# Alpha as ScalarE's partition scale in a fused attention and snake MLP, in place of scaled weights

## The chip, the cores and the metric

The kernel runs on one core of one Trainium2 chip. The metric is the device time of one execution in microseconds (us), as the median of several runs. The *profiled span* is the length of one profiled execution; it is about 2 us shorter than the time of the same run. Line numbers (L372) belong to the kernel whose profile is shown: L489 of the kernel before and L472 of the changed one are the same matmul.

## The reference

```python
# attention with keys and values averaged over 8 rows, 8 batches, 8 heads, 576 rows, head 64
scores = scale * q @ mean8(k).T;  attn = softmax(scores);  x = attn @ mean8(v)     # x: 4608 x 512
# the MLP: w_in 512 x 2048, w_out 2048 x 512, alpha: 2048
h = x @ w_in
s = sin(alpha * h)
g = h + s * s / (alpha + 1e-9)
out = g @ w_out
```

All is float32. Alpha belongs to a column of h; in the kernel h lies transposed, so alpha belongs to a partition.

## The kernel before

Both matmuls of the MLP are cut into 2x2 blocks and done with seven products in place of eight (a Strassen form), which needs sums of blocks of x, w_in and w_out. The first matmul runs in nine *units* of 512 tokens. A unit has four groups J of seven products, 28 *slots*; in each slot the instructions listed for it go ahead of that slot's product on every engine, and the attention of the next batch is laid into the slots this way. The second matmul (the *output stage*) follows from about 560 us to the end.

The kernel before folds alpha into the weights. With w_in' = w_in * alpha the product is alpha*h at once. The sine then needs alpha/(alpha + 1e-9), and w_out is divided by alpha + 1e-9, so that the square can be plain.

```python
    def combine_alpha(self):
        ...                                  # al: alpha by partition
        for c in range(4):                   # alb: alpha in the free dimension, on all partitions
            nc.tensor.matmul(ps[:], self.ones[:], self.al_row[:, s], start=True, stop=True)
            nc.scalar.activation(out=self.alb[:, s], in_=ps[:], func=AF.Identity, ...)
        # ral = 1 / (al + 1e-9),  rat = al * ral
    def combine_w_in(self, J, part):         # VectorE, in slots of the first unit (J = 0: before it)
        def scaled(t, i):
            nc.vector.tensor_tensor(out=t[:, :, s], in0=t[:, :, s], in1=c, op=OP.mult)    # L372
        ...                                  # four scaled() and four sums for each J
    def load_w_out(self, wp):
        ...
                    nc.vector.tensor_scalar(out=t[:, k], in0=t[:, k], scalar1=self.ral[:, f:f + 1], ...)  # L408
    # one group's pieces, run one slot behind its products 1, 5, 6, 2, 7, 3, 4
            def left0(G=G, Q=before):        # after product 1
                nc.scalar.copy(out=G.b6[:], in_=G.b1[:])                    # L507
                if Q and not early(Q):
                    squares(Q)               # of the group before: 128x512 and 128x1024
            ...
            def left2(G=G, Q=before):        # after product 6
                nc.scalar.copy(out=G.b7[:], in_=G.b6[:])                    # L519
                nc.scalar.copy(out=G.p5[:], in_=G.b5[:])
            def left3(G=G):
                sin(G, 0, 0, G.b1)
                square(G, G.s[:, 0, 0])
            ...
```

The copies L507 and L519 put a partial sum into the bank to which a later product adds: TensorE waits for them if they are late. Five banks rotate.

## Time and profile before

| | kernel before |
|---|---|
| time | 958.22 us (957.25 to 960.15) |
| profiled span | 956.4 us |
| busy: TensorE, VectorE, ScalarE, GpSimd | 937.6, 676.5, 414.2, 197.7 us |
| values matmul of the first batch begins | 34.62 us |
| second unit's long stretch begins | 130.03 us |
| from unit to unit after that | 57.20 us |
| output stage begins | 560.43 us |

The prediction below shows the rows of this profile that it rests on. Two views are needed beside them. The first is the chain of waits in the steady part (start, length, what; x144 is the number of matmuls). Each unit from the second on has one stretch of 18 products, 144 matmul records, with nothing of the attention between them; it serves as a clock mark:

```profile
187.23 31.32 PE bank L489 x144
...
462.11 45.17 PE bank L489 x208
...
560.43 4.62 PE bank L752 x40
```

187.23 less the 130.03 of the unit before is 57.20, the length of a unit. The second view is TensorE's timeline between 40 and 100 us, of which these are the matmuls that waited (start, length, what, and in brackets the wait and what ended it):

```profile
44.41 1.97 PE L489 MATMUL bank<-home,as 128*128 128x256 f32 x8 [1.64 <-DVE as L368]
...
49.48 1.99 PE L489 MATMUL bank<-home,a 128*128 128x256 f32 x8 [1.39 <-ACT bank L519]
...
55.75 0.44 PE L177 MATMUL ps_kt<-ident,kp 72*128 72x72 f32 x4 [0.81 <-ACT aT L269]
...
80.92 1.99 PE L489 MATMUL bank<-home,as 128*128 128x256 f32 x8 [1.00 <-ACT bank L507]
...
97.39 1.14 PE L267 MATMUL ps_at<-ident,ex 128*72 128x128 f32 x8 [2.02 <-DVE aT L269]
```

With the wait of 1.62 at 89.89, which the prediction shows, the six come to 8.5 us.

### The profile page before, as it was taken

The page shows a single profiled execution, that of the slowest core. Times are in us where ns is not written, and L with a number is a line of the kernel's source. Part 1 is how long each engine was busy: PE and PEld are TensorE (multiplying, and loading weights), DVE is VectorE, ACT ScalarE, POOL GpSimd, SP SyncE. Part 2 cuts the span into 40 slices and gives each one's busy share as a digit, 9 for nine tenths or more (in the row PEclk, how much of TensorE's full clock was granted, in tenths as well). Part 3 has the DMA queues.
Part 4 walks back from the last instruction along what each step waited for, and adds up shares of the span by engine and source line. Part 5 has one row for each costly group of instructions (what it writes and reads, how often), then busy time and mean ns, then how long its engine had stood idle before and what let it go on. Part 6 is the DMA issues. An engine that isn't in the chain of part 4 may idle for free.

```text
span 956.4 us, 18152 instructions
## 1 busy us (share of the span) xinstructions
PE 937.6 (98%) x7259; PEld 833.4 (87%) x7259; DVE 676.5 (71%) x1070; ACT 414.2 (43%) x919; POOL 197.7 (21%) x215
## 2 busy tenths in 40 slices
PE   7998999999999999999999999999999999999998
PEld 3677687887878878787888899999999999999998
DVE  5889585766838577483576996867768695958684
ACT  5376466575756747566555531111111111111111
POOL 1717364443724436260000000000000000000000
PEclk9999999999999999999999999999999999999999
DMA  9636466666576663745615235324142434343201
GB/s 222 176 104 198 125 195 142 205 149 196 171 198 201 156 190 102 188 136 161 242 54 206 98 142 190 125 102 161 67 155 78 143 115 147 98 139 122 100 34 35
DMA packets 84038, 137.88 MB, mean 144 GB/s; under 512 B 10177, under 2 KB 49873, under 8 KB 79345
## 3 DMA queue, kind: packets, MB, share of 16 engines
q1 hardware_dynamic: 83920, 136.70, 47.1%
q8 instruction: 58, 0.95, 0.4%
q14 instruction: 26, 0.21, 0.1%
q10 hardware_dynamic: 34, 0.02, 0.0%
HBM read 74.47 MB, written 47.19 MB: 127 GB/s over the span
## 4 chain that ended last, share of the span: by engine, by line
PE 92%; DVE 4%; ACT 2%; DMA 1%; issue 0%; SPq 0%; DVEq 0%; ACTq 0%
PE bank L489 42%; PE bank L752 30%; PE ps_y L752 12%; PE ps_o L309 3%; PE ps_sc L208 2%; DMA q<-in_q_dram 1%; DVE as L368 1%; ACT s L495 1%; PE ps_at L267 1%; DVE home L462 1%; DVE a L372 1%; PE ps_qt L189 1%; PE bank L452 1%; DVE h L468 0%; PE ps_or L318 0%
## 5 line engine op out<-in xcount | busy, mean ns | idle before, releaser
L489 PE MATMUL bank<-home,a 128*128 128x256 f32 x1152 | 266.3, 382 | 3.0 <-DVE h L468 1.6
L489 PEld LDWEIGHTS bank<-home,a 128*128 128x128 f32 x1152 | 215.3, 190 | 36.6 <-DVE h L468 3.1
L489 PE MATMUL bank<-home,as 128*128 128x256 f32 x864 | 201.6, 382 | 2.8 <-DVE as L368 1.6
L489 PEld LDWEIGHTS bank<-home,as 128*128 128x128 f32 x864 | 161.7, 190 | 26.7 <-ACT bank L507 2.4
L105 POOL TENSOR_TENSOR kvin<-kvin 72x512 f32<-72x512 f32 x112 | 126.0, 1125 | 180.3 <-DMA kvin<-in_v_dram 112.0
L495 ACT ACTIVATE s<-h,rat 128x256 f32<-128x256 f32 x144 | 65.2, 500 | 90.2 <-DVE h L468 90.2
L468 DVE TENSOR_TENSOR h<-bank,p 128x512 f32<-128x512 f32 x72 | 49.1, 682 | 74.7 <-ACT s L497 47.4
L752 PE MATMUL bank<-wb,home 128*128 128x128 f32 x712 | 92.1, 275 | 0.0
L752 PEld LDWEIGHTS bank<-wb,home 128*128 128x128 f32 x712 | 85.7, 192 | 0.0
L831 ACT COPY bank<-bank 128x128 f32<-128x128 f32 x63 | 15.8, 250 | 149.3 <-PE bank L752 149.2
L497 ACT ACTIVATE s<-s 128x512 f32<-128x512 f32 (+1 forms) x106 | 77.8, 768 | 1.1
L495 ACT ACTIVATE s<-bank,rat 128x256 f32<-128x256 f32 x144 | 59.9, 467 | 36.9 <-PE bank L489 24.4
L752 PE MATMUL bank<-wb,xe 128*128 128x128 f32 x512 | 67.6, 275 | 0.0
L752 PEld LDWEIGHTS bank<-wb,xe 128*128 128x128 f32 x512 | 62.4, 192 | 0.1
L844 ACT COPY bank<-bank 128x128 f32<-128x128 f32 x63 | 15.8, 250 | 96.6 <-PE bank L752 96.6
L250 POOL TENSOR_TENSOR ex<-ex,sm 128x576 f32<-128x576 f32 (+1 forms) x38 | 42.5, 1148 | 46.5 <-DVE sm L249 21.4
L549 DVE TENSOR_TENSOR h<-h,s 128x1024 f32<-128x1024 f32 x36 | 44.5, 1237 | 0.0
L549 DVE TENSOR_TENSOR h<-bank,s 128x512 f32<-128x512 f32 x36 | 24.5, 681 | 24.5 <-ACT s L497 23.9
L819 ACT COPY bank<-ps_y 128x256 f32<-128x256 f32 x63 | 22.5, 357 | 35.9 <-PE ps_y L752 35.9
L519 ACT COPY bank<-bank 128x512 f32<-128x512 f32 x36 | 20.6, 571 | 39.4 <-PE bank L489 39.4
L712 DVE TENSOR_TENSOR xe<-home 128x512 f32<-128x512 f32 x30 | 19.4, 687 | 25.5 <-PE bank L752 25.4
L215 DVE TENSOR_REDUCE mx<-ps_sc 128x4 f32<-128x288 f32 (+1 forms) x75 | 33.6, 448 | 4.4 <-PE ps_sc L208 4.4
(152 smaller groups left out, 1499.3 us busy)
## 6 DMA issues: line engine op xcount, KB each, us to landing
g_bridge<-h SPq DMA_DIRECT2D x36, 1024.0 KB
r<-g_bridge SPq DMA_DIRECT2D x18, 1024.0 KB
home<-g_bridge SPq DMA_DIRECT2D x18, 1024.0 KB
out_dram<-o SPq DMA_DIRECT2D x36, 256.0 KB
q<-in_q_dram SPq DMA_DIRECT2D x8, 1024.0 KB
kvin<-in_k_dram SPq DMA_DIRECT2D x28, 288.0 KB
kvin<-in_v_dram SPq DMA_DIRECT2D x28, 288.0 KB
a<-in_moe_w_in_dram SPq DMA_DIRECT2D x16, 256.0 KB
```

The costliest lines, as they stand in the source:

```text
L105: (eng or nc.gpsimd).tensor_tensor(out=o, in0=t[:, :, 0:w], in1=t[:, :, w:2 * w], op=OP.add)
L215: nc.vector.tensor_reduce(out=mx[:n], in_=ps[:n], axis=AX, op=OP.max)
L250: eng.tensor_tensor(out=E(n, i, 0, H), in0=E(n, i, 0, H), in1=sm[:n].unsqueeze(2).to_broadcast([n, H, Sp]), op=OP.mult)
L309: nc.tensor.matmul(ps[64 * e:64 * e + 64, :], vp[:, h, :], x, start=True, stop=True)
L468: add = lambda o, x, y: nc.vector.tensor_tensor(out=o, in0=x, in1=y, op=OP.add)
L489: nc.tensor.matmul(ps[:, jj, :], self.A[p][:, kk, f * P:(f + 1) * P], x[:, kk, :], start=(start and jj == 0 and kk == 0), stop=(kk == 1), ...
L495: nc.scalar.activation(out=G.s[:, i, j, jj, :], in_=src[:, jj, :], func=AF.Sin, scale=self.rat[:, f:f + 1])
L497: square = lambda G, x: nc.scalar.activation(out=x, in_=x, func=AF.Square)
L519: nc.scalar.copy(out=G.b7[:], in_=G.b6[:])
L549: add = lambda o, x, y: nc.vector.tensor_tensor(out=o, in0=x, in1=y, op=OP.add)
L752: nc.tensor.matmul(out, A[:, J, :], W[:, J // 2, J % 2, :], start=(start and J == 0), stop=(J == self.NJ - 1), skip_group_check=True)
L819: nc.scalar.copy(out=x[:, 0:2, :], in_=yz[:, 0:1, :].to_broadcast([P, 2, P]))
```

## The change

Its intent is to take 48 scalings of weights off VectorE and the spreading of alpha off TensorE, and to have ScalarE apply alpha inside instructions that it runs anyway. The sine takes alpha as its scale. The square takes c = 1/sqrt(alpha + 1e-9) as its scale, since (c*s)^2 = s*s/(alpha + 1e-9). A partition scale holds for one block of 128 columns of w_in only, so a square that went over two or four such blocks is cut. Slots move to make room.

```diff
-        # combine_alpha: four ones-by-row matmuls, four evictions into alb; ral; rat
+    def root(self):
+        ts(a, self.al[:], 1e-9, OP.add, 1.0, OP.mult)
+        nc.vector.reciprocal(out=t, in_=a)
+        nc.scalar.activation(out=c, in_=t, func=AF.Sqrt)
+        ...                                             # one Newton step: c *= 1.5 - 0.5 * c * c * a
 # combine_w_in
-        (four scaled() for each J)
+        (in the groups J = 2 and 3 the first of the four sums moves from slots 12 and 20 to slots 10 and 14,
+         where their scalings stood)
 # load_w_out
-                    nc.vector.tensor_scalar(out=t[:, k], in0=t[:, k], scalar1=self.ral[:, f:f + 1], ...)
 # a group's pieces
-   ... func=AF.Sin, scale=self.rat[:, f:f + 1])
+   ... func=AF.Sin, scale=self.al[:, f:f + 1])
-            square = lambda G, x: nc.scalar.activation(out=x, in_=x, func=AF.Square)
+            def square(G, i, js):
+                for jj in range(JW):
+                    x = G.s[:, i, js, jj, :]
+                    nc.scalar.activation(out=x, in_=x, func=AF.Square, scale=self.c[:, f:f + 1])
 # slots of the first unit
-            at(6, A.k_t)
+            at(7, A.k_t)
-                at((7, 8, 9, 11, 13)[i], A.score, i)
-                at(15 + (i + 1) // 2, A.exp, i)
-                at((16, 17, 17, 18, 19)[i], A.norm, i)
+                at((8, 9, 10, 11, 13)[i], A.score, i)
+                at((15, 16, 17, 17, 17)[i], A.exp, i)
+                at((16, 17, 18, 18, 19)[i], A.norm, i)
 # slots of the later units
-                at(8 + (i + 1) // 2, A.exp, i)
-                at(9 + (i + 1) // 2, A.norm, i)
+                at((8, 9, 10, 10, 10)[i], A.exp, i)
+                at((9, 10, 11, 11, 12)[i], A.norm, i)
 # (cut: one square moved ahead of the last sine pair in the early group; names and tiles of alpha)
```

More of the change, by code (lines that the diff above doesn't have):

```diff
@@ L321, in attention, with load_alpha, turn_alpha @@
         return SimpleNamespace(**{f.__name__: f for f in (k_t, q_t, score, exp, score_exp, norm, new_a, a_t, turn, move, values, values_rest)})
-    def load_alpha(self, row, rows):
+    def load_alpha(self, rows):
         nc = self.nc
         self.al = self.const.tile([P, self.K2], F32, name="al")
-        self.ral = self.const.tile([P, self.K2], F32, name="ral")
-        self.rat = self.const.tile([P, self.K2], F32, name="rat")
-        self.alb = self.new_tr()[:, 0:self.FF]
-        self.al_row, self.al_rows = row[0:1], rows[:self.K2]
+        self.c = self.const.tile([P, self.K2], F32, name="c")
+        self.al_rows = rows[:self.K2]
         nc.scalar.dma_start(out=self.al_rows, in_=self.alpha.rearrange("(k p) -> k p", p=P))
-        nc.scalar.dma_start(out=self.al_row, in_=self.alpha.rearrange("(o n) -> o n", o=1))
-    def combine_alpha(self):
+    def turn_alpha(self):
         nc = self.nc
@@ L340, in combine_alpha @@
         nc.scalar.copy(out=self.al[:], in_=ps[:])
-        for c in range(4):
-            s = slice(512 * c, 512 * c + 512)
-            ps = self.bank([P, 512], c)
-            nc.tensor.matmul(ps[:], self.ones[:], self.al_row[:, s], start=True, stop=True)
-            nc.scalar.activation(out=self.alb[:, s], in_=ps[:], func=AF.Identity, bias=self.ex[:, 0, 0, self.Sp:self.Sp + 1])
-        nc.vector.tensor_scalar(out=self.ral[:], in0=self.al[:], scalar1=1e-9, scalar2=None, op0=OP.add)
-        nc.vector.reciprocal(out=self.ral[:], in_=self.ral[:])
-        nc.vector.tensor_tensor(out=self.rat[:], in0=self.al[:], in1=self.ral[:], op=OP.mult)
+    def root(self):
+        nc, c = self.nc, self.c[:]
+        a, t = (self.const.tile([P, self.K2], F32, name=n)[:] for n in ("a", "t"))
+        tt = lambda o, x, y: nc.vector.tensor_tensor(out=o, in0=x, in1=y, op=OP.mult)
+        ts = lambda o, x, p, f, q, g: nc.vector.tensor_scalar(out=o, in0=x, scalar1=p, scalar2=q, op0=f, op1=g)
+        ts(a, self.al[:], 1e-9, OP.add, 1.0, OP.mult)
+        nc.vector.reciprocal(out=t, in_=a)
+        nc.scalar.activation(out=c, in_=t, func=AF.Sqrt)
+        tt(t, c, c)
+        tt(t, t, a)
+        ts(t, t, -0.5, OP.mult, 1.5, OP.add)
+        tt(c, c, t)
     def load_w_in(self):
@@ L368, in combine_w_in @@
         tt = lambda o, x, y, op: nc.vector.tensor_tensor(out=o[:, :, s], in0=x[:, :, s], in1=y[:, :, s], op=op)
-        def scaled(t, i):
-            c = self.alb[:, i * h + J * w:i * h + (J + 1) * w].unsqueeze(1).to_broadcast([P, 2, w])
-            nc.vector.tensor_tensor(out=t[:, :, s], in0=t[:, :, s], in1=c, op=OP.mult)
-        if J < 2:
-            if part == 0:
-                scaled(a11, 0)
-                scaled(a21, 1)
-                scaled(a22, 1)
-                tt(s1, a21, a22, OP.add)
-            else:
-                tt(s2, s1, a11, OP.subtract)
-                scaled(a12, 0)
-                tt(a21, a11, a21, OP.subtract)
-                tt(s4, a12, s2, OP.subtract)
-        elif part == 0:
-            for t, i in ((a11, 0), (a21, 1), (a22, 1), (a12, 0)):
-                scaled(t, i)
+        if part == 0:
+            tt(s1, a21, a22, OP.add)
         else:
-            tt(s1, a21, a22, OP.add)
             tt(s2, s1, a11, OP.subtract)
@@ L404, in load_w_out @@
             yield
-            for t, i in ((b11, 0), (b12, 0), (b22, 1), (b21, 1)):
-                for k in range(c, c + 2):
-                    f = i * kk + k
-                    nc.vector.tensor_scalar(out=t[:, k], in0=t[:, k], scalar1=self.ral[:, f:f + 1], scalar2=None, op0=OP.mult)
             s = slice(c, c + 2)
@@ L494, in sin @@
                     f = i * self.K2 // 2 + G.J * JW + jj
-                    nc.scalar.activation(out=G.s[:, i, j, jj, :], in_=src[:, jj, :], func=AF.Sin, scale=self.rat[:, f:f + 1])
-            square = lambda G, x: nc.scalar.activation(out=x, in_=x, func=AF.Square)
+                    nc.scalar.activation(out=G.s[:, i, j, jj, :], in_=src[:, jj, :], func=AF.Sin, scale=self.al[:, f:f + 1])
+            def square(G, i, js):
+                for jj in range(JW):
+                    f = i * self.K2 // 2 + G.J * JW + jj
+                    x = G.s[:, i, js, jj, :]
+                    nc.scalar.activation(out=x, in_=x, func=AF.Square, scale=self.c[:, f:f + 1])
             early = lambda G: G.J == (0 if G.u else 1)
             def squares(G):
-                square(G, G.s[:, 0, 1])
-                square(G, G.s[:, 1])
+                if not early(G):
+                    square(G, 0, 1)
+                square(G, 1, slice(0, 2))
+            self.squares = squares
             def left0(G=G, Q=before):
@@ L507, in left0 @@
                 nc.scalar.copy(out=G.b6[:], in_=G.b1[:])
-                if Q and not early(Q):
+                if Q:
                     squares(Q)
@@ L524, in left3 @@
                 sin(G, 0, 0, G.b1)
-                square(G, G.s[:, 0, 0])
+                square(G, 0, 0)
             def left4(G=G):
@@ L536, in left6 @@
                 sin(G, 0, 1, G.g[:, 0, 1])
+                if early(G):
+                    square(G, 0, 1)
                 sin(G, 1, 0, G.b7)
-                if early(G):
-                    squares(G)
             self.left = [(left0, left1, left2, left3, left4, left5, left6)[k]]
@@ L547, in finish @@
     def finish(self, Q):
-        nc = self.nc
-        add = lambda o, x, y: nc.vector.tensor_tensor(out=o, in0=x, in1=y, op=OP.add)
+        add = lambda o, x, y: self.nc.vector.tensor_tensor(out=o, in0=x, in1=y, op=OP.add)
         add(Q.g[:, 1, 0], Q.b7[:], Q.s[:, 1, 0])
@@ L559, in end_hidden @@
             f()
-        nc.scalar.activation(out=Q.s[:, 0, 1], in_=Q.s[:, 0, 1], func=AF.Square)
-        nc.scalar.activation(out=Q.s[:, 1], in_=Q.s[:, 1], func=AF.Square)
+        self.squares(Q)
         self.finish(Q)
@@ L572, in first_batch @@
         h = [self.hp.tile([P, 4 * POOL * self.D], F32, name="h") for _ in range(2)]
-        self.load_alpha(h[1][:], self.hp.tile([P, P], F32, name="s", bufs=1)[:])
-        self.combine_alpha()
+        self.load_alpha(self.hp.tile([P, P], F32, name="s", bufs=1)[:])
+        self.turn_alpha()
         for i in range(4):
             self.load_kv("k", 0, i, nc.vector, at=far[i // 2][:self.Sp, i % 2])
+        self.root()
         self.load_q(0)
@@ L858, in run @@
             make_identity(nc, ident)
-            self.ones = const.tile([1, P], F32, name="ones")
-            nc.gpsimd.memset(self.ones[:], 1.0)
             engines = {nc.tensor.engine, nc.vector.engine, nc.scalar.engine, nc.gpsimd.engine, nc.sync.engine}
```

## The prediction

> **What bounds the kernel now.** I read the page's busy shares first, then its slices:
>
> ```profile
> PE 937.6 (98%) x7259; PEld 833.4 (87%) x7259; DVE 676.5 (71%) x1070; ACT 414.2 (43%) x919; POOL 197.7 (21%) x215
> ...
> PE   7998999999999999999999999999999999999998
> ```
>
> TensorE is busy 98% of the span; 956.4 - 937.6 = 18.8 us is all the idle time it has. A change that gives TensorE no less work to do can win only there, plus the few places where "busy" hides a stalled pipe. So the second view is where that idle time lies, by stretches (columns: length, then busy us of PE, PEld, DVE, ACT, POOL):
>
> ```profile
> 0.00:25.00 25.00, 19.06 (x142) 10.08 (x143) 12.66 (x34) 13.28 (x42) 3.49 (x11) 1.00 0.90 219
> 25.00:50.00 25.00, 21.75 (x169) 15.94 (x168) 20.65 (x33) 9.98 (x31) 16.35 (x14) 1.00 0.67 189
> 50.00:75.00 25.00, 24.19 (x265) 19.44 (x264) 21.80 (x41) 16.04 (x32) 2.94 (x4) 1.00 0.37 108
> 75.00:100.00 25.00, 20.36 (x103) 16.83 (x102) 24.00 (x35) 17.70 (x31) 21.68 (x21) 1.00 0.58 165
> 100.00:150.00 50.00, 50.00 (x395) 39.79 (x393) 36.63 (x62) 30.82 (x62) 25.75 (x29) 1.00 0.52 152
> ```
>
> 14.6 us of the 18.8 are in the first 100 us; 3.5 more are the tail after 900 us. From 100 to 900 us TensorE has nothing to gain. In 75-100 VectorE is busy 24.0 of 25: there it sets the pace. Third view, the chain of waits followed back from the end, in its first 135 us (start, length, what):
>
> ```profile
> 2.48 11.04 DMA q<-in_q_dram
> ...
> 35.11 1.81 DVE a L372 x3
> ...
> 44.26 1.13 DVE a L372
> ...
> 68.34 2.40 DVE a L372 x4
> ...
> 130.03 31.32 PE bank L489 x144
> ```
>
> L372 is the scaling of w_in by alpha, which goes. It holds 1.81 + 1.13 + 2.40 = 5.3 us of the chain. Until 13.5 us the chain is the load of q; at 130 us it is pure matmul: 144 records in 31.32 us, 217 ns each, the rate of a full pipe.
>
> **What the Trainium skill says.** "ScalarE: Activation LUTs", section What ACT_TABLE_LOAD costs: each [128,1] pointer operand adds about 93 ns to an ACTIVATE, and back-to-back ones overlap by about 93 ns. The trace agrees: a sine with a pointer scale on 256 elements takes 500 ns from SBUF, where the two Square sizes below, without pointer, put 256 elements at 421. The same section gives 1283 ns for a table load and 1380 ns of drain on top; the trace has the 1283 exactly but no drain (a load at 192.00, the first exp at 193.29). The section Table sets: Exp and Sqrt are in different sets, so the new Sqrt brings loads of its own. "TensorE: Matmul & The Clock Gate", Part 1: the array starts at half rate and is let go after about 3.4 us of activity. Here the transposes of q run at 246 ns each from 14.02 (8 in 1.97 us) and at about 150 from 19.07 (4 in 0.59 us), so it woke near 18 us; the 7.2 us of one-row alpha matmuls before did not wake it (0.86 us per 512 columns throughout).
>
> **The change part by part.** The groups it touches, with busy us and mean ns:
>
> ```profile
> L495 ACT ACTIVATE s<-h,rat 128x256 f32<-128x256 f32 x144 | 65.2, 500 | 90.2 <-DVE h L468 90.2
> L497 ACT ACTIVATE s<-s 128x512 f32<-128x512 f32 x71 | 44.7, 630 | 1.1
> L497 ACT ACTIVATE s<-s 128x1024 f32<-128x1024 f32 x35 | 36.7, 1048 | 0.0
> L372 DVE TENSOR_TENSOR a<-a,tr 128x512 f32<-128x512 f32 x16 | 12.7, 842 | 0.0
> L408 DVE TENSOR_SCALAR wb<-wb,ral 128x256 f32<-128x256 f32 x32 | 8.7, 347 | 0.0
> ```
>
> *Removed, VectorE:* 16 scalings of w_in, 12.7 us, all between 35 and 84 us, where TensorE does wait; 32 scalings of w_out, 8.7 us, between 450 and 560 us, where TensorE is full: worth nothing. *Removed, TensorE:* eight records that spread alpha over the partitions, 7.2 us busy, before q is there at 13.5 us: worth nothing (the busy share will fall without gain). Their four evictions on ScalarE, 4 x 0.69 us, are also ahead of q.
>
> *Added at the start:* a Sqrt, a table load for it and one more for Exp (1.28 us each), seven tiny VectorE operations of about 0.2 us. VectorE ends the k sums at 11.4, so the root is ready near 13.1 with Sqrt's load long done: ahead of q. The Exp load falls at 16.6 to 17.9, and the first exp waited for its maximum until 17.8 anyway: 0.1 us at most.
>
> *Added on ScalarE:* squares are cut by partition scale. Per group, 630 + 630 + 1048 becomes four of 128x256 at about 500 and two of 128x512 at 630 + 93. Less overlaps, 2.2 us become about 4 x 0.41 + 2 x 0.63 = 2.9. Over 36 groups that is 24 us; ScalarE should read 435 to 445 us.
>
> *Moved:* one square goes ahead of the last sine pair, exps bunch differently, first-batch scores go one slot later and k's transpose moves from slot 6 to 7.
>
> **Does the extra ScalarE work cost in the steady part?** The tight place is the exp group, in the third unit:
>
> ```profile
> 191.39 0.59 ACT L507 COPY bank<-bank 128x512 f32<-128x512 f32 x1
> 192.00 1.28 ACT L225 ACT_TABLE_LOAD   x1
> 193.29 1.83 ACT L225 ACTIVATE ex<-ex 128x576 f32<-128x576 f32 x3
> 195.03 0.58 ACT L519 COPY bank<-bank 128x512 f32<-128x512 f32 x1
> ```
>
> The L519 copy ends at 195.61; by counting 217 ns records on from 187.23, the product that needs it starts at 195.94. In the new order the L507 copy no longer stands behind the squares, so it can begin when its product lands, about 190.95. Then: copy to 191.45, two squares to 192.75, load to 194.0, two exps to 195.2, copy to 195.7. A slack of 0.33 shrinks to about 0.2 but stays. The next eviction of that kind I get at 204.2 against a need at 204.6. I allow 0.3 us over all seven such units.
>
> **The walk through the first 100 us.** I step the same instructions on with the row durations, without the scalings.
> - To 44.2: no gain. The sums of x wait for x itself (38.9 us, from TensorE and ScalarE), so dropping three scalings before them only makes VectorE wait.
> - At 46.8 the last score tile's maximum comes 1.1 us sooner (one scaling of a12 less ahead of it), and with it its exps and the copy that frees the second product: gain 1.1.
> - 50 to 62: ScalarE is solid with copies, sines, squares and now sets the pace; with k's transpose out of slot 6, TensorE no longer waits to 55.75 for a buffer. The next group's first product starts about 57.0 instead of 59.9; longer squares then hold an eviction, and the third product starts near 63.5 to 64.1 instead of 65.9: gain about 2.
> - 66 to 82: four scalings (2.49 us) leave the score queue, but the exps now meet the squares on ScalarE; the product at 84.55 starts near 82.3 to 82.8: gain 2.
> - 84 to 97: here it pays most.
>
> ```profile
> 79.47 4.56 DVE L372 TENSOR_TENSOR a<-a,tr 128x512 f32<-128x512 f32 x4
> ...
> 89.89 1.99 PE L489 MATMUL bank<-home,a 128*128 128x256 f32 x8 [1.62 <-DVE h L468]
> ```
>
> Four scalings take 4.56 us while GpSimd works beside them; the norms and the add behind them come late, and TensorE waits. Without them the add is done near 86 and this product starts at about 86: gain 3.7.
> - 92 to 97: the last sums of w_in (4.8 us) still stand ahead of VectorE's copy of the transposed attention (done 97.25 before), and ScalarE's squares ahead of its copy. I get 94 to 94.5: gain about 3.3. From there TensorE is full as before.
>
> Sum: -3.3 at the start, +0.3 in the steady part: -3.0. The outputs from 560 us are pure TensorE and do not change. Prediction 958.2 - 3.0 = 955.2 us.
>
> **The rivals.** (1) The chain's full share is won, 5.3 us, or even the idle time of 34 to 98 us, about 8.6 us in the waits: 950 to 953. For it: VectorE is what TensorE waits for at 89.89 and 97.35. Against it: ScalarE takes over in 50-62, and no chain share is won whole when the wait behind it is close. (2) ScalarE becomes the bound in the exp groups: +0.6 us in each of 7 units gives back 4 us and the time is the same or 1 us longer, about 959. For it: slack of only 0.2 by my count. Against it: the early square and the bunched exps were evidently placed to keep that slack. (3) The clock gate: without the alpha matmuls the array wakes later, up to one window of 3.4 us at half rate, at most 1.5 us. Against it: those matmuls didn't wake it before either.
>
> **Range and chances.** Walking errors are about 2 us either way and the runs before spread over 2.9 us: 951.5 to 958. A 2% change would be 19 us, more than all of TensorE's idle time, and for a loss ScalarE would have to hold up every group by half a microsecond. Faster 0.01, same 0.98, slower 0.01.
>
> **What would show it.** VectorE near 654 us busy, ScalarE near 440, TensorE near 930 with the same span from 100 us on: units still 57.2 us apart. The matmul waits at 89.89 and 97.35 shorter or gone; 50-62 ScalarE solid. Wrong if TensorE shows new waits for ScalarE's copies between 100 and 560 us (rival 2), or if the first 34 us differ by over 1 us (rival 3).

## The result, and the profile after

| | before | after |
|---|---|---|
| time, median (range) of 4 runs each | 958.06 (957.25 to 960.15) | 953.72 (952.8 to 954.76) |
| ratio, 95% interval | | 0.9952 (0.9933 to 0.9971): within 2% |
| profiled span | 956.4 | 952.0 |
| long stretch of the second unit begins | 130.03 | 123.47 |
| from unit to unit | 57.20 | 57.45 |
| output stage begins | 560.43 | 555.81 |

The result lies inside the range, 1.5 us under the predicted 955.2. The table also shows that two terms of the sum were off: the start gained more than was predicted, and the part after it gave more back.

First the busy row of the changed kernel's page:

```profile
PE 932.7 (98%) x7251; PEld 830.2 (87%) x7251; DVE 659.0 (69%) x1025; ACT 440.2 (46%) x1026; POOL 199.7 (21%) x214
```

TensorE is still busy 98% of the span. VectorE lost 17.5 us and ScalarE gained 26.0, and the span moved by a quarter of the one and a sixth of the other: neither sum says anything of the time by itself.

Next the stretches from 25 to 100 us (length, then busy us of PE, PEld, DVE, ACT, POOL; granted clock, DMA share and GB/s), which answer to those in the prediction:

```profile
25.00:50.00 25.00, 23.73 (x183) 17.38 (x182) 19.08 (x32) 12.37 (x34) 13.92 (x14) 1.00 0.67 196
50.00:75.00 25.00, 25.00 (x265) 20.58 (x264) 20.11 (x35) 15.97 (x37) 8.42 (x8) 1.00 0.50 146
75.00:100.00 25.00, 23.18 (x123) 17.76 (x122) 20.87 (x32) 20.35 (x41) 21.73 (x22) 1.00 0.52 163
```

TensorE is busy 71.9 of these 75 us; before it was 66.3. The 5.6 us between are the start's gain, seen as idle time that has been filled. VectorE, 24.0 of 25 in the last row before, is at 20.9 there.

The timeline of TensorE shows which waits they were. These are the ones left between 40 and 100 us:

```profile
43.11 1.97 PE L472 MATMUL bank<-home,as 128*128 128x256 f32 x8 [0.79 <-DVE as L371]
...
47.06 1.99 PE L472 MATMUL bank<-home,a 128*128 128x256 f32 x8 [0.25 <-ACT bank L510]
...
80.69 1.99 PE L472 MATMUL bank<-home,a 128*128 128x256 f32 x8 [0.59 <-ACT bank L510]
...
90.93 1.14 PE L267 MATMUL ps_at<-ident,ex 128*72 128x128 f32 x8 [1.20 <-DVE aT L269]
```

They come to 2.8 us where there were 8.5. The wait for a buffer at 55.75 and the one for VectorE's add at 89.89 are gone; the product of the latter now begins at 84.26.

The chain shows what was given back after that (start, length, what):

```profile
123.47 31.57 PE bank L472 x144
...
180.93 31.57 PE bank L472 x144
...
457.06 45.17 PE bank L472 x208
...
555.81 4.73 PE bank L742 x40
```

The same 144 matmuls take 31.57 us where they took 31.32, and a unit is 180.93 - 123.47, rounded 57.45, where it was 57.20. So the lead is 6.56 us at the second unit's stretch, 5.05 at the stretch of 208, and 4.62 where the outputs begin. The 0.25 us a unit are lost in and just behind the exp group, at three weight loads that wait. In the third unit (timeline of ScalarE, and of TensorE's weight loads in the last three lines):

```profile
185.10 1.33 ACT L485 ACTIVATE s<-s,c 128x512 f32<-128x512 f32 x2
186.45 1.28 ACT L225 ACT_TABLE_LOAD   x1
187.74 1.26 ACT L225 ACTIVATE ex<-ex 128x576 f32<-128x576 f32 x2
188.91 0.58 ACT L510 COPY bank<-bank 128x512 f32<-128x512 f32 x1
...
189.53 1.59 PEld L472 LDWEIGHTS bank<-home,a 128*128 128x128 f32 x8 [0.18 <-ACT bank L510]
...
193.10 3.32 PEld L472 LDWEIGHTS bank<-home,a 128*128 128x128 f32 x16 [0.25 <-DVE h L451]
...
198.41 1.59 PEld L472 LDWEIGHTS bank<-home,as 128*128 128x128 f32 x8 [0.27 <-ACT bank L498]
```

The kernel before has one such wait in the same stretch:

```profile
199.29 3.32 PEld L489 LDWEIGHTS bank<-home,a 128*128 128x128 f32 x16 [0.18 <-DVE h L468]
```

What each costs the matmuls is seen from their begins in TensorE's timeline, counted from the first of the stretch (180.86 after, 187.16 before). Behind the first wait the next product begins at 10.51 us (191.37), where it began at 10.47 (197.63). Behind the second it is 15.80 (196.66) against 15.69 (202.85), and behind the third 19.39 (200.25) against 19.14 (206.30). So the copy of L510 accounts for 0.04 of the 0.25, VectorE's add of L451 for 0.07, and the copy of L498 for 0.14. It is the same in each of the six units.

The slack at the copy of L510 can now be estimated. It ends at 189.49, 8.56 us after the begin of the stretch in the chain; before it ended at 8.38 (195.61 - 187.23, from the lines in the prediction). It came 0.18 later and cost 0.04, so the slack of the kernel before was about 0.14 us and not 0.33. The matmul may be due at 8.71, but its weight load goes ahead of it and waits for the bank too.

Last, the begin of the output stage. In the kernel before, the chain there is matmul after matmul. In the changed one it goes by the last squares and the small copy behind them:

```profile
553.87 1.72 ACT s L485 x3
555.59 0.17 ACT bank L834
```

From the stretch that begins at 505.75 (510.81 before) to the outputs it is 50.06 us where it was 49.62, a loss of 0.44. By the output matmuls at 568.90 (573.09 before) 0.43 more are lost, and 0.26 come back where the kernel before has a wait of its own, near 731 us. With six units at 0.25 the whole is 6.56 - 1.51 - 0.44 - 0.43 + 0.26 = 4.44 us, where the spans differ by 956.4 - 952.0 = 4.4.

Of the 6.56 at the start, 0.44 are put down to chance and not to the change: the first values matmul began at 34.18 and not 34.62, because the load of q landed sooner, and among the runs below, the alpha row apart, that matmul begins anywhere between 33.4 and 36.0.

### The profile page after: what moved, and what is told of

Same layout as the page of the kernel before. It is cut to its first block, busy times and chain, and to the rows that moved or that the text cites. A ratio compares the mean times of both kernels' runs of the same rounds, so it can differ in the third digit from the quotient of the medians. Undisturbed runs are those within 1.5% of the kernel's fastest.

```text
span 952.0 us, 18201 instructions
## 1 busy us (share of the span) xinstructions
PE 932.7 (98%) x7251; PEld 830.2 (87%) x7251; DVE 659.0 (69%) x1025; ACT 440.2 (46%) x1026; POOL 199.7 (21%) x214
## 4 chain that ended last, share of the span: by engine, by line
PE 95%; ACT 2%; DVE 1%; DMA 1%; issue 0%; SPq 0%; DVEq 0%; ACTq 0%
PE bank L472 45%; PE bank L742 30%; PE ps_y L742 12%; PE ps_o L309 3%; PE ps_sc L208 2%; DMA q<-in_q_dram 1%; PE ps_qt L189 1%; PE ps_at L267 1%; PE bank L435 1%; ACT s L478 0%; DVE as L371 0%; DVE home L445 0%; PE ps_or L318 0%; PE bank L120 0%; PE bank L208 0%
## 5 line engine op out<-in xcount | busy, mean ns | idle before, releaser
L105 POOL TENSOR_TENSOR kvin<-kvin 72x512 f32<-72x512 f32 x112 | 123.8, 1105 | 163.5 <-DMA kvin<-in_v_dram 107.8
L485 ACT ACTIVATE s<-s,c 128x256 f32<-128x256 f32 (+1 forms) x216 | 110.0, 572 | 0.0
L478 ACT ACTIVATE s<-h,al 128x256 f32<-128x256 f32 x144 | 65.2, 501 | 82.0 <-DVE h L451 82.0
L451 DVE TENSOR_TENSOR h<-bank,p 128x512 f32<-128x512 f32 x72 | 49.0, 680 | 63.5 <-ACT s L485 28.1
L478 ACT ACTIVATE s<-bank,al 128x256 f32<-128x256 f32 x144 | 59.9, 467 | 36.0 <-DVE h L539 9.5
L145 DVE STREAM_TRANSPOSE tr<-q 128x1024 f32<-128x1024 f32 (+1 forms) x24 | 18.1, 808 | 26.8 <-DMA aT<-tr 21.3
L216 DVE TENSOR_TENSOR ex<-ps_sc,mx 128x288 f32<-128x288 f32 (+1 forms) x75 | 34.2, 456 | 2.9
```

The costliest lines, as they stand in the source:

```text
L105: (eng or nc.gpsimd).tensor_tensor(out=o, in0=t[:, :, 0:w], in1=t[:, :, w:2 * w], op=OP.add)
L216: nc.vector.tensor_tensor(out=ex[:n, i, e::2, 0:Sp], in0=ps[:n], in1=mx[:n].unsqueeze(2).to_broadcast([n, NP, Sp]), op=OP.subtract)
L451: add = lambda o, x, y: nc.vector.tensor_tensor(out=o, in0=x, in1=y, op=OP.add)
L478: nc.scalar.activation(out=G.s[:, i, j, jj, :], in_=src[:, jj, :], func=AF.Sin, scale=self.al[:, f:f + 1])
L485: nc.scalar.activation(out=x, in_=x, func=AF.Square, scale=self.c[:, f:f + 1])
```

## The experiments

The question is not whether the prediction's sum was right but why it was: what brought 6 us at the start in place of 3.3, and what gave back more than 0.3. The theories:

- A: the w_in scalings on VectorE carry the start gain. B: the moved slots or the lost alpha row carry it.
- C: the longer, cut squares cost the steady 0.25 us a unit and the wait at the outputs; the rival is the new slot order.
- E: the gain is larger than the walk because VectorE and GpSimd slow each other, so that a scaling costs more than its own row; the rival is that each scaling just delays what is behind it by its row.

To keep the chance of the start out, I quote for each run the *start length*: from the begin of the first values matmul to the begin of the second unit's long stretch. It was 95.41 us before and 89.29 after, so the gain proper is 6.1 us.

| run | time (range) | ratio (95%) | start length | a unit or its x144 stretch |
|---|---|---|---|---|
| before | 958.06 | 1 | 95.41 | 57.20; 31.32 |
| after | 953.72 | 0.9952 | 89.29 | 57.45; 31.57 |
| w_in scalings back | 959.99 (959.29-961.2) | 1.0009 (0.999-1.0029) | 95.49 | 57.45; 31.57 |
| first half of them back | 955.6 (955.31-955.89) | 0.9967 (0.9951-0.9984) | 91.73 | x144 31.57 |
| alpha row back | 956.38 (956.29-957.51) | 0.9973 (0.9954-0.9992) | 89.27 | 57.45 to 57.8; 31.57 |
| before, GpSimd short | 952.15 (951.79-952.99) | 0.9929 (0.9915-0.9944) | 89.08 | x144 31.32 |
| after, GpSimd short | 951.2 (950.76-951.89) | 0.9922 (0.9905-0.9939) | 86.55 | x144 31.57 |
| after, old slots | 958.78 (958.34-959.34) | 0.9996 (0.9977-1.0014) | 89.57 | 57.95 to 58.2 |
| before, new slots | 957.37 (955.67-959.4) | 0.9983 (0.9955-1.0011) | 95.13 | 57.16; 31.28 |
| after, whole squares | 952.7 (951.01-953.26) | 0.9931 (0.9915-0.9946) | 88.66 | 57.18; 31.30 |
| w_out scalings back | 955.59 (955.38-956.2) | 0.9965 (0.9951-0.9979) | 89.36 | about 57.5 |
| exps bunched, early copy | 956.58 (955.6-957.03) | 0.9972 (0.9959-0.9986) | 88.78 | 57.7 to 58.0 |
| more reordering | 953.62 (952.87-956.54) | 0.995 (0.9932-0.9968) | 88.88 | 57.5 to 57.7; 31.28 |
| one exp between the copies | 954.58 (952.77-955.56) | 0.9955 (0.994-0.997) | 89.5 | 57.2 to 57.6; 31.28 |

### The w_in scalings put back, by ones

```diff
 # the changed kernel
+        self.alb = self.new_tr()[:, 0:self.FF]
+        nc.gpsimd.memset(self.alb, 1.0)
 # combine_w_in: as in the kernel before, with its four scaled() for each J
```

> The changed kernel with the 16 scalings of w_in put back on VectorE in their old places, by ones, so the result stays right. Theory A (VectorE's scalings held TensorE up in the first 100 us): most of the start gain goes; the matmul block of the second unit, which begins at 123.47 us in the changed kernel and 130.03 before, begins at 127 to 130 us, and the time is 957 to 960 us. Theory B (the moved slots and the missing row of alpha made the start shorter): it stays within 1.5 us of 123.5, time 953 to 955.

The start length is 95.49, that of the kernel before, and all else is the changed kernel. The chain has both marks at once, the late begin and the longer stretch:

```profile
129.68 31.57 PE bank L490 x144
```

Theory A holds: what was put back is worth 6.2 us at the start, more than the scalings' chain share of 5.3 and less than half of their 12.7 us of busy time. The run is not faster than the kernel before, so the rest of the change, taken together, wins nothing.

This run puts back one thing more than the scalings. The first sum of the last two groups is again behind them, as before. For the last group that is seen at the last wait of the start, the one for VectorE's copy of the transposed attention: in the kernel before four sums stand ahead of that copy, and in the changed one the first is done long ago. Before, then after:

```profile
91.81 1.16 DVE L368 TENSOR_TENSOR as<-a,a 128x512 f32<-128x512 f32 x1
```

```profile
75.60 0.67 DVE L371 TENSOR_TENSOR as<-a,a 128x512 f32<-128x512 f32 x1
```

TensorE's wait there is 2.02 us before and in this run, and 1.20 us in the changed kernel. So about 0.8 of the 6.2 go with the moved sum. This is read from the waits; no run has the move alone.

### Only the first eight put back

```diff
 # as above, but
         elif part == 0:
-            for t, i in ((a11, 0), (a21, 1), (a22, 1), (a12, 0)):
-                scaled(t, i)
+            tt(s1, a21, a22, OP.add)
         else:
-            tt(s1, a21, a22, OP.add)
             tt(s2, s1, a11, OP.subtract)
```

> The changed kernel with only the first eight scalings of w_in put back (the first two column groups, run between 35 and 57 us), by ones. All sixteen took the start from 89.3 us (from the first product with v to the second unit's block) to 95.5. If the loss is shared as VectorE's time is, the first half takes about half, 92 to 93; if it is the four scalings beside GpSimd near 80 us that matter, as the wait at 89.89 us said, the first half costs at most 1.5, 89.3 to 91.

The start length is 91.73, between the two stated ranges. The first eight bring 2.4 us, so the other eight, with the moved sums, the remaining 3.8. The waits at the third and fifth product of x return (1.63 and 1.39 us); those after 80 us are the changed kernel's. The gain is thus spread over the whole start, with the greater part in the later half, where VectorE was busy 24 of 25 us.

### The alpha row put back

```diff
 # the changed kernel: load of alpha as a row, and in turn_alpha
+        for c in range(4):
+            nc.tensor.matmul(ps[:], self.ones[:], self.al_row[:, s], start=True, stop=True)
+            nc.scalar.activation(out=self.alb[:, s], in_=ps[:], func=AF.Identity, ...)
```

> The changed kernel with the row of alpha back at the start: its load, eight one-row matmul records, four evictions. In the changed kernel q arrived 0.67 us sooner and the first x product began 0.45 us sooner. If the row's load or its matmuls cost that, q's first transposes begin near 14.0 us (13.36 changed, 14.02 before) and the time is 0.5 us longer; if it was chance, they begin anywhere from 13.3 to 14.1 and the time is the changed kernel's, 953 to 954.5.

Neither number came. The start length is 89.27, so the row changes nothing behind the first values matmul, but that began at 37.11, some 2.9 us late. The timeline of ScalarE shows how:

```profile
13.22 1.28 ACT L354 ACT_TABLE_LOAD   x1
```

The row's evictions keep ScalarE until 13.21, so the load of Sqrt's table comes only then and the root's Newton step ends at 15.56 on VectorE. VectorE's copies of q stand behind that step and begin at 15.48, where they began at 12.87 in the changed kernel. So this is a collision of the row with the root, which neither kernel has, and it does not measure the row. That the row by itself costs nothing is seen from other runs that still have it: in the kernel before with new slots the first values matmul began at 33.89, earlier than the changed kernel's 34.18.

### The kernel before with short sums on GpSimd (wrong result)

```diff
 # the kernel before, load_kv
+        if b == 1:
+            nc.gpsimd.tensor_tensor(out=to[b][...], in0=t[:, :, 0:D], in1=t[:, :, D:2 * D], op=OP.add)
+            return
         for w in (4 * D, 2 * D, D):
```

> The kernel before, with GpSimd's sums of k and v of batch 1 cut to one small add each (the result is wrong on purpose). Theory E (VectorE's operations of 34 to 47 and 75 to 85 us run at up to 2.5 times their length because GpSimd works beside them, so that the scalings cost more than 0.68 us each): all scalings take 0.68 to 0.70 us, VectorE's time of 34 to 47 us shrinks by 3 to 5 us, and the second unit's block begins at 125 to 128 us instead of 130. Theory F (they are slow because of the loads that land then): durations stay, block begins at 129 to 130.5.

This kernel keeps all sixteen scalings and drops most of GpSimd's work on the keys and values of the second batch, which GpSimd does while VectorE is at the scalings. Its relative error is 0.30, as it should be. Its start length is 89.08, 6.3 us less, about what the change wins (6.1). The long stretch begins at 125.03, as theory E said. The Trainium skill's page "SBUF — State Buffer", section "Who interferes with whom", says that a VectorE instruction with two SBUF inputs contends with a GpSimd instruction that reads SBUF. The trace agrees. First the kernel before (duration in ns, least, median and most, then first and last start):

```profile
L372 DVE TENSOR_TENSOR a<-a,tr x16: 676/682/1750, 35.0 to 82.8; 128x512 f32<-128x512 f32 x16
```

And the same line of code with GpSimd's sums cut:

```profile
L375 DVE TENSOR_TENSOR a<-a,tr x16: 673/678/686, 36.4 to 78.5; 128x512 f32<-128x512 f32 x16
```

A scaling takes 0.68 us alone and up to 1.75 beside GpSimd. It is not always VectorE that is held up: the first three scalings took 0.68 us each (from 35.03) beside a pair of GpSimd's sums that took 4.08, where a pair took 2.07 in the steady part. And it is not the scalings alone. In the kernel before, one of the sums of x, also with two SBUF inputs, took 1.57 us while GpSimd was at a pair of its own (timeline of VectorE, then of GpSimd):

```profile
39.02 1.57 DVE L462 TENSOR_TENSOR home<-home,home 128x512 f32<-128x512 f32 x1
...
38.33 2.84 POOL L105 TENSOR_TENSOR kvin<-kvin 72x512 f32<-72x512 f32 x2
```

In the changed kernel the sum in the same place took 0.79, but the next but one took 1.75, so the sharing is not gone there. This sum and the three instructions behind it show best what it does, since no scaling stands among them: to the end of the w_in sum for which the third product of x waits, they take 5.24 us in the kernel before and with the scalings put back, 4.46 in the changed kernel, and 2.50 in both kernels with GpSimd's sums cut. The rival, that a scaling only delays what is behind it by its row, can't be the whole: when the scalings go, GpSimd's sums fall beside other instructions.

### The changed kernel with the same cut (wrong result)

```diff
 # the changed kernel, load_kv: the same three lines
```

> The changed kernel with GpSimd's sums of batch 1 cut to one small add each (wrong on purpose), as in e8_short_gpsimd for the kernel before, where the start fell from 95.4 to 89.1 us. If the sharing between VectorE and GpSimd was what made VectorE late, and the scalings only added to it, the changed kernel gains much less from it: 86.5 to 88.5 instead of 89.3. If it gains the same 6 us, the two are independent.

The start length is 86.55, so the cut is worth 2.7 us here and was worth 6.3 in the kernel before. Read the other way, the change is worth 89.08 - 86.55 = 2.5 us when GpSimd is short and 6.1 when it is not. The two do not add, but this alone does not show theory E. TensorE's waits in the start of the kernel before come to 8.5 us, less than the 12.4 us that the two gains would make together, and this run has a single wait of 1.2 us left. Two gains that empty the same waits can't add, sharing or not. What shows the sharing is the durations above; how much of the 6.1 us hangs on it stays open. The cut also has the sums of k and v ready sooner and lets GpSimd come sooner to its part of the norms, and I have no run that separates this from the sharing itself.

### The moves of slots: out, and alone

```diff
 # (1) the changed kernel with the slots of before: k_t 6; score (7, 8, 9, 11, 13); exp and norm
 #     by (i + 1) // 2 in both kinds of units
 # (2) the kernel before with the slots of after
```

> The changed kernel with k's transpose, the scores, exps and norms back in their old slots. Theory A: the second unit's block begins by 125 us, time 953 to 955.5. Theory B: 126 to 130 us, time 956 to 959. For the 0.25 us a unit that the steady part lost: with three exps instead of two ahead of the copy that the fifth product needs, that wait grows by about 0.6 us in each of six units, so units are 57.8 to 58.1 us apart (57.45 in the changed kernel, 57.20 before) if it is ScalarE's queue that costs there, and unchanged if not.

> The kernel before with only the moves of slots (k's transpose, scores, exps, norms). Theory A: with the scalings still there it gains at most 2 us, the second unit's block begins at 128 to 130 us, time 956 to 959. Theory B: begins at 124 to 126, time 952 to 954.5. Units stay 57.2 us apart, since its squares are the short ones.

At the start the moves are worth 0.3 us in either direction (89.57 against 89.29; 95.13 against 95.41). So theory B falls, though the time with the old slots, 958.78, is outside theory A's range. In the steady part the moves matter: with the old slots and the new squares the stretch of 208 begins at 460.50 in place of 457.06, 3.4 us later, and about 1 us more is lost by the end. The table of waits from 130 to 560 us (us in total, times, longest) has for the six units:

```profile
PEld bank L472 <- ACT bank L510: 4.5, 6, 0.8
```

So the moves are what keeps the longer squares affordable: they prevent about 0.6 us a unit, and 0.25 remains. In the kernel before, with its short squares, the same new slots have the unit at 57.16, no worse than the old: the new order by itself is not what costs.

### Whole squares in the changed kernel

```diff
             def square(G, i, js):
-                for jj in range(JW): ... scale=self.c[:, f:f + 1]
+                x = G.s[:, i, js]
+                nc.scalar.activation(out=x, in_=x, func=AF.Square)
```

> The changed kernel with every square in one piece and without a pointer scale, in the changed kernel's places (the result is wrong on purpose). Theory C (the longer squares cost the 0.25 us in each of six units and the 0.45 us where the outputs begin): units come back to 57.20 us or a little less, ScalarE falls to about 415 us, and the time is 951 to 952.5. Theory D (the moved exps or the order of the early square cost it): units stay near 57.45 and the time 953 to 954.5.

This leaves out the division by alpha and was meant to give a wrong result. It passed the comparison all the same, presumably because the attention's averaged values make h, and with it the square of the sine, small; I did not measure that. ScalarE is busy 416.0 us, about as before, and the chain has the short stretch again:

```profile
122.52 31.30 PE bank L472 x144
```

Units are 57.18 apart but for one of 57.54, the wait at the outputs is gone (they begin at 553.17), and the span is 948.9 against 952.0. Of the three weight loads above only the one for the later copy (L498, here L495) still waits, 0.16 us. Theory C holds by the units, though the median time of 952.7 lies between the two stated ranges and the profiled execution, of 951.01, was the fastest of four. Of the 3.1 us of span between the two profiled executions, 0.6 are in the start length and 0.3 in the chance of the start, 1.25 in the steady part, and 0.9 from the begin of the outputs on. By the ratios, 0.9931 against 0.9952, the difference is about 2 us. The run takes away the cutting and the pointer scale at once and does not tell them apart. What the squares take by form is (busy us, mean ns):

```profile
L485 ACT ACTIVATE s<-s,c 128x256 f32<-128x256 f32 x144 | 64.9, 502 | 0.0
...
L485 ACT ACTIVATE s<-s,c 128x512 f32<-128x512 f32 x72 | 47.7, 713 | 0.0
```

These are of the changed kernel; the prediction had 500 and 723.

### The w_out scalings put back, by ones

```diff
 # the changed kernel
+        self.ral = self.const.tile([P, self.K2], F32, name="ral");  nc.gpsimd.memset(self.ral[:], 1.0)
 # load_w_out: the 32 tensor_scalar of before
```

> The changed kernel with the 32 scalings of w_out back on VectorE, by ones. The prediction says they are worth nothing: same as the changed kernel within 0.5 us, 953 to 954.5, VectorE 8.5 us busier. The rival says that they delay the eviction work between 450 and 560 us: 1 us or more slower.

They are not quite free here. From the begin of the stretch at 411.60 to that at 507.27 it takes 95.67 us, against 95.02 in the changed kernel, and TensorE waits for a VectorE add in that time (two waits, 1.0 us). That is 0.65 of the span's 1.6; 0.57 is the chance of the start, and the rest I did not trace. In the kernel before, the scalings stood in the same place and the stretch took 94.78, with no such wait. So removing them won nothing, as was predicted, but the changed order could no longer have carried them for nothing.

### Three attempts at a better order

```diff
 # (1) the changed kernel
-                at((8, 9, 10, 10, 10)[i], A.exp, i);   at((9, 10, 11, 11, 12)[i], A.norm, i)
+                at((8, 10, 10, 10, 10)[i], A.exp, i);  at((9, 11, 11, 12, 12)[i], A.norm, i)
 #     and the outputs' first small copy goes ahead of the last squares
 # (2) as (1), with the block transposes at (13, 13, 13, 14, 14), the first unit's exps at
 #     (15, 17, 17, 17, 17), norms at (16, 18, 18, 19, 19), and the last sums of w_in in two parts
 # (3) as (2), with the second exp between the two copies of slot 10, and one load of k later
```

> The changed kernel with two of its new waits taken away by order alone: in the steady units only one exp ahead of the copy that the fifth product needs (its norm later too), and the last group's squares behind the outputs' first small copy. Theory C or not, if ScalarE's queue is what costs, units fall from 57.45 to about 57.2 us (1.5 us in six units) and the wait of 0.4 to 0.6 us before the first outputs goes: 951.5 to 952.5, about 1.5 to 2 us under the changed kernel. If units stay at 57.45, the wait is elsewhere.

The wait for L510 and nearly all of that at the outputs (0.2 us left) are gone, but a unit is longer, not shorter. VectorE's norms now come behind the block transposes, an add comes late (196.69 us), and the next group's copy of L498 keeps TensorE's weight loads for 4.3 us in eight waits (2.6 us in the changed kernel). A miss: the order that frees ScalarE loads VectorE at a worse moment.

> e6_fixed lost because its norms and transposes kept VectorE from the add that the next sines need. This has its exps and its earlier copy, but the block transposes of the scores one slot later, behind that add; the same exps in the first unit; and the last sums of w_in split, so that two of them come after the copies of the transposed attention. If ScalarE's copy and VectorE's add are all that hold the units up, they come to 57.15 to 57.25 us (57.45 in the changed kernel), the start shortens by 0.5 to 1.5 us, and the time is 1.5 to 3.5 us under the changed kernel's: 950 to 952.5. If units stay above 57.4, a third wait is there.

The stretch of 144 is back at 31.28 us, and the start length is 88.88. But units are 57.5 to 57.7: the first values product of each unit comes 0.2 to 0.5 us late, in two of them with the wait put down to the transfer of the turned attention. The time is that of the changed kernel.

> e10_reordered brought the nine-product stretch of a unit to 31.28 us (31.57 in the changed kernel, 31.32 before), but its transposes ended later and TensorE then waited for the turned attention to land, so units were 57.2 to 57.7 us apart. Here the second exp runs between the two copies, so its norm starts 0.5 us sooner, and one load of k stands behind the moves in the queue. If that late landing was the third wait, units come to 57.1 to 57.25 us, and the time to 949.5 to 951.5; if they stay above 57.4, the cause is another.

The stretch is 31.28 again, and the values products are on time. Two of five units take 57.16; the others take 57.4 to 57.6, and what they have more lies in one tile's score products. Its time is no better than that of the changed kernel. So I have no correct version that beats it; what the cut squares cost was moved about and not removed by order alone.

## Why the prediction was right or wrong

The range (951.5 to 958) and the reason were right: TensorE is full, and only the first 100 us have idle time to win. Point by point:

- **The sum.** It said -3.3 at the start and +0.3 in the steady part. Measured: -6.1 at the start, +1.5 over six units, +0.4 where the outputs begin and +0.4 just behind. Both terms were too small, with opposite signs, so that the sum was off by only 1.5 us. That the total came so near is luck.
- **The walk through the first 100 us** is the term most mis-sized. The mechanism was right: the scalings carry most of it (6.2 us when put back, about 0.8 of it with the moved sum). Its steps were short nearly from the first. "To 44.2: no gain" was 0.9 (44.41 to 43.11, less the chance 0.44); the "gain 1.1" was 2.0; the next group's first product was to start at 57.0 and did at 55.5, and its third at 63.5 to 64.1 and did at 61.4, since no square held an eviction there; the product of 84.55 was to start at 82.3 to 82.8 and did at 80.7; that of 89.89 at about 86, and did at 84.3; the transposes were to be at 94 to 94.5 and were at 90.9.
- **Why it was short.** "I step the same instructions on with the row durations" took the durations of the kernel before for what is left on VectorE. They are not its own, since they hold the time for which GpSimd's sums held it up. "To 44.2: no gain" is the clearest case: the four instructions ahead of that product took 4.46 us and not 5.24 with no scaling among them, nearly all of the 0.9. Each later step starts from there. At the end, "the last sums of w_in (4.8 us) still stand ahead" missed that the edit takes one of the four away: three stood there, from 86.46 to 90.19, and the wait for VectorE's copy was 1.20 in place of 2.02. How the rest divides is not shown.
- **Rival 1** (8.6 us or 5.3) was nearer for the start than the prediction itself. The reason given against it, that ScalarE takes over in 50 to 62 us, held in part only: there is no TensorE idle time left in 50 to 75 us at all.
- **The steady part.** "A slack of 0.33 shrinks to about 0.2 but stays" was wrong. By the estimate above it was about 0.14, the copy came 0.18 later, and 0.04 was lost. The size of the squares was right (502 and 713 ns); the count of slack put the end of the copy against the begin of a matmul and left out its weight load. The greater part, 0.21 of the 0.25 us a unit, was lost at two places that got no such count: VectorE's add, which the walk does not mention here, and the next eviction, "at 204.2 against a need at 204.6". Counted on the times of the kernel before, that copy ended at 204.7. This is the prediction's own sign of rival 2, new waits for ScalarE's copies, at 0.25 us a unit and not 0.6; the 0.6 is what the old slots cost.
- **"The outputs … do not change"** was wrong by about 0.9 us: the last group's squares stand ahead of the output stage's first small copy. Whole squares do away with it.
- **Rival 3**, the clock gate, did not come about: the score matmuls at the start fall from 0.32 to 0.22 us by 18.33 us, and by 18.52 in the kernel before.
- **The busy sums** were right: ScalarE 440.2 us (435 to 445), TensorE 932.7 (near 930), and VectorE 659.0 (near 654) a little high.
- **Removing the w_out scalings and the alpha row is worth nothing:** right. The root's two table loads came at 4.08 and 15.97, and the first exp began 0.15 us after its maximum, where it was 0.04 before: the 0.1 that was allowed.

## What to carry to other kernels

When work leaves an engine, don't step the rest on with the old durations: instructions that shared something with another engine have that engine's time in their rows, and what is left will fall beside other work. Look also for what the edit moves without saying so, such as a sum that takes the place of the scalings. A slack of a few tenths of a microsecond, counted by hand, should be counted to the weight load as well as the matmul, and at every wait near it; the loss here was spread over three. When two changes each win time and together win less than their sum, ask first how much idle time there was to win. A partition scale makes a removed scaling cheap, but it cuts wide instructions into as many as there are scales; that price is paid in every unit, while the gain here came only once.

## What the Trainium skill lacked or had wrong

- "SBUF — State Buffer" says which VectorE and GpSimd instructions contend, which is right here, but nothing on what this makes of a kernel. A 128x512 product of two SBUF tiles took 0.68 us alone and up to 1.75 us beside GpSimd's sums, and the four instructions ahead of the third product took 2.50 us with GpSimd's sums cut, and 4.46 or 5.24 beside them, as they happened to fall.
- "ScalarE: Activation LUTs" adds a drain of 1380 ns to a table load. The load took 1.28 us here as it says, and there was no such time on either side of it: the last square ends at 186.43, the load begins at 186.45, and the exp begins at 187.74.
- "TensorE: Matmul & The Clock Gate" has the array woken by activity; 7.2 us of one-row matmuls in the kernel before stayed at 0.86 us per 512 columns, where 256 columns take 0.216 us in the steady part (half the time per column), and the page does not say what counts as activity.
- How late a weight load may come before its matmul waits: I found it on none of the pages that I read. Where nothing waits (the kernel before with new slots), the load begins 0.21 us ahead of its matmul. Loads that came 0.13, 0.15, 0.15, 0.22 and 0.24 us later than that (five waits in three kernels) delayed the matmuls by 0.02, 0.04, 0.04, 0.11 and 0.13 us, so that about 0.11 us was free each time. One such load began 0.04 us after the end of the copy it waited for.
